# The last stores of a two-branch FNet and MLP layer: whole sets of four on one queue, the last chunk undivided, one sum moved behind a split

## The chip, the cores and the metric

The kernel runs on one core of one Trainium2 chip. The metric is the device time of one execution in microseconds (us); lower is better. The kernel before takes 862.84 us, the median of 3 runs (862.46 to 862.95).

## The reference: what is computed

For x of 2048 rows and 640 columns in float32, a layer norm feeds two branches, and all three terms are added:

```
xn = layernorm(x)
a, b = xn @ dft_hid_re.T, xn @ dft_hid_im.T
y = x + (dft_seq_re @ a - dft_seq_im @ b) + (gelu(xn @ w1 + b1) @ w2 + b2)
```

w1 is 640 by 1536, w2 is 1536 by 640, the sequence matrices are 2048 by 2048 and the hidden ones 640 by 640. All matrices are inputs, so the Fourier part is done with matmuls.

## The kernel before

**Numbers.** Every float32 operand is split into a high and a low part (`split`, lines 153 to 160): ScalarE copies the value into a rounded high part, VectorE subtracts that from the value to get the low part. A product is three matmuls (`product`, lines 268 to 273): high by high (line 271), high by low (line 272), low by high (line 273), accumulated in one PSUM bank. The weight operand is the stationary one, the split operand made by `form` (lines 490 to 504) the moving one, 512 columns wide.

**Stages.** First comes the MLP with the layer norm, over four blocks t of 512 rows. Its result plus x is kept in DRAM (`ys`). Then come the sequence stages, one for each of eight blocks (half h, rows t), and after every second block of the second half one hidden stage ("y") for a pair of row blocks `ta`, `tb`. Both kinds of stage form a product of 2 by 2 blocks with seven products (`NW = 7`) in place of eight. The last hidden stage is the end of the kernel; its pair is ta = 1, tb = 2.

**A hidden stage** has 21 entries n, seven products w by three units u. For each entry the main loop (lines 1229 to 1244) records the matmuls (`hidden_entry`, lines 1181 to 1223), then the functions in `pre`, then `form(n + 3)`, which splits the moving operand of the third entry from there, then the functions in `post`. Every engine runs its own instructions in that recorded order (`manual_schedule`). `hidden_beside` (lines 1053 to 1161) says what stands in `pre` and `post` of each entry.

In the last stage the last product (w = 6) is laid out differently (lines 1194 to 1204). Entry 18 holds 15 matmuls into bank VS (five positions of three) and then 15 into bank X; entry 19 holds 15 into bank X + 1; entry 20 holds none. Bank X already holds the sum after w = 5. That sum is read by VectorE at entry 17: `v1 += x_` (line 1123, recorded at line 407, 128x1024 over banks X and X + 1). The 15 matmuls into VS read the splits of entries 18, 19 and 20, two positions each of the first two and one of the third; the split for entry 20 is half as wide (128x512) and is the last form of the kernel.

**The results of the last stage** leave in this order. `out_b(0)` and `out_b(1)` (line 1115) store columns 0 to 63 and 64 to 127 of each quarter of block tb, from tiles `u`; `yb4` (line 1119) stores the odd 32 columns of tb from tile `y`; and after the main loop (lines 1252 to 1262) the third and fourth chunk of 32 columns of block ta leave tile `yo`. Each time VectorE turns a PSUM bank or a sum in 32 by 32 pieces (lines 842, 845, 1260) and adds the turned tile to what is in SBUF (line 407).

**A store** is `store` (lines 820 to 825): four DMAs, one for each quarter q of the partitions and of the columns. With `both` false all four are issued by SP (`nc.sync`), with `both` true the first two by SP and the last two by ACT (`nc.scalar`). Before the change `out_b(0)` goes to SP, all that follow use both. The last chunk is turned, added and stored in two halves of its row groups (`n0`, `n1`), each in four DMAs of 32 KB; the other stores of 32 columns are four of 64 KB, those of 64 columns four of 128 KB.

**Semaphores of DMAs.** Each DMA gets one of eight completion semaphores, here called 0 to 7. A DMA that gets one that was used before waits, in its queue, until the DMA that had it has landed; what is queued behind it on that engine waits as well. As the program is built, the last stores have these semaphores, in the order of each queue:

| store | SP before | ACT before | SP after | ACT after |
|---|---|---|---|---|
| `u`, columns 0 to 63 | 0, 1, 3, 5 | - | 0, 1, 3, 5 | - |
| `u`, columns 64 to 127 | 7, 2 | 2, 4 | - | 2, 4, 6, 1 |
| `y`, odd columns | 6, 1 | 6, 0 | 7, 0, 2, 3 | - |
| `yo`, third chunk | 2, 3 | 1, 3 | - | 4, 6, 0, 1 |
| `yo`, fourth chunk, first half | 4, 5 | 4, 5 | - | - |
| `yo`, fourth chunk, second half | 6, 7 | 7, 0 | - | - |
| `yo`, fourth chunk whole | - | - | 5, 7 | 2, 3 |

Where both queues of the kernel before have a semaphore in the same row (2, 6, 3, 4, 5, 7), the store on ACT has it first and that on SP waits for it; the SP store of `y` with semaphore 1 waits for the first `yo` store on ACT.

Of the kernel before, what the change touches and what calls it, by code (L numbers as in the profile page):

```python
# [16 lines left out]
Q = 4  # L17
B = 32
# [7 lines left out]
def kernel(  # L26
# [38 lines left out]
    nc = tc.nc  # L65
    x = x.flatten_outer_dims()
    out = out.flatten_outer_dims()
# [4 lines left out]
    NB = TB // B  # L72
# [4 lines left out]
    DQ = D // Q  # L77
# [27 lines left out]
    def bank(k):  # L105
        return banks[:, k]
# [35 lines left out]
    def place(tag, shape, dtype=F32R):  # L142

        return wpool.tile(list(shape), dtype, tag=tag, bufs=1, name=tag)
# [24 lines left out]
    def rows_of(ap, t):  # L169
        return ap[t * TB : (t + 1) * TB].rearrange("(n r) d -> r n d", r=B)  # L170
# [162 lines left out]
    A = {}  # L333
# [72 lines left out]
    def add(dst, a, b, op=ALU.add):  # L406
        nc.vector.tensor_tensor(dst, a, b, op=op)  # L407
# [23 lines left out]
    def load_a(g):  # L431

        for f in steps_of_load(g):
            f()
# [71 lines left out]
    def f5(u):  # L506
        add(held("ci1", u), held("ci1", u), held("ci2", u))

    def f6(u):
        add(held("cr1", u), held("cr1", u), held("ci1", u))  # L510
# [104 lines left out]
    for tag, size, keys in PLACES:  # L615
        t = place(tag, (P, size // 4))
# [13 lines left out]
    last = 1  # L630
# [99 lines left out]
    for g in range(NG):  # L730
        t, i = divmod(g, NF)
# [73 lines left out]
    def load_part(t, k):  # L805
        nc.sync.dma_start(new_sum(1, t, k), part_of(t, k))

    def gather(h, t, k, acc, first=False, op=ALU.add):

        if h == 0 and first:  # L810
            nc.scalar.activation(new_sum(h, t, k), acc, AF.Copy, scale=-1.0 if op == ALU.subtract else 1.0)
        else:
            add(sums[t, k], sums[t, k], acc, op)
# [3 lines left out]
            for k in names:  # L817
                nc.sync.dma_start(part_of(t, k), sums[t, k])

    def store(t, src, c0, c1, both=False, n0=0, n1=NB):  # L820

        for q in range(Q):
            (nc.scalar if both and q > 1 else nc.sync).dma_start(
                rows_of(out, t)[:, n0:n1, q * DQ + c0 : q * DQ + c1], src[q * B : (q + 1) * B, n0:n1]
            )

    def reload(lo, w, which="xab"):
# [10 lines left out]
    def turned(acc, name):  # L838

        if len(acc.shape) == 2:  # L840
            yt = A["yt"](name)[:, 0]
            nc.vector.transpose(yt, acc)
        else:
            yt = A["yt"](name)
            nc.vector.transpose(yt.rearrange("p e n -> p (e n)"), acc.rearrange("p e n -> p (e n)"))
        return yt

    def add_turned(dst, yt):
        if len(yt.shape) == 2:
            add(dst, dst, yt.rearrange("p (n i) -> p n i", i=B))  # L850
        else:
            d = dst.rearrange("p n (e i) -> p e n i", i=B)
            add(d, d, yt.rearrange("p e (n i) -> p e n i", i=B))
# [14 lines left out]
    X, Y, Z, US, VS = 0, 3, 5, 2, 7  # L868
    yo = {}
# [166 lines left out]
    def load_g(b, i):  # L1036
        if i >= NW * ND:
            return
        w, c = G[i]
        n = GWIDE[w] * P  # L1040
        places = A["g", b]
        k = i % len(places)
        if b < len(blocks) - 1 and w == NW - 1:

            k = (i - 2) % len(places)
            if c in CHUNKS[0]:
                k = CHUNKS[0].index(c)
                places = {k: fr_tile((P, 6 * P), f"u{2 - k}_{sets[blocks[b]]}", f"gr{k}_{b}", F32R)}
        g = places[k][:, : 2 * n].rearrange("p (a b) -> p a b", a=2)
        GT[b, i] = g  # L1050
        nc.sync.dma_start(g.bitcast(F32), wits[w][c])

    def hidden_beside(b, n):


        ta, tb = blocks[b - 1][1], blocks[b][1]
        last = b == len(blocks) - 1
        x_, y_, z_ = (banks[:, k : k + 2] for k in (X, Y, Z))
        us, vs = bank(US), bank(VS)
        ya = yo[ta]  # L1060

        def s(which, k):
            return sums[(ta, tb)[which], k]

        def t2(k):
            return lambda: add(s(1, KU[k]), s(1, KV[k]), s(1, KU[k]), ALU.subtract)

        def t3(k):
            return lambda: add(s(0, KU[k]), s(1, KU[k]), s(0, KU[k]), ALU.subtract)

        def t4(k):
            return lambda: add(s(0, KV[k]), s(0, KV[k]), s(1, KU[k]), ALU.subtract)

        def columns(k):

            return s(1 if last else 0, ("u1", "u2")[k]).rearrange("p a b -> p (a b)").rearrange("p (n e) -> p n e", n=NB)

        def load_yb(k):
            return lambda: nc.sync.dma_start(columns(k), ys[k][tb])

        def copy(dst, src):
            return lambda: nc.scalar.activation(dst, src, AF.Copy)

        def to(dst, acc, name, then=lambda: None):


            def f():
                add_turned(dst, turned(acc, name))
                then()

            return f

        def out_a(c0, c1):
            return lambda: store(ta, ya[:, :, c0:c1], c0, c1) if last else None

        def odd():
            yt = turned(us, f"yo_{tb}")
            add_turned(ya[:, :, 4 * B :], yt)
            add_turned(yo[tb, 4], yt)
            out_a(4 * B, DQ)()  # L1100

        def in_two(k):

            acc, name = s(1, ("v2", "v1")[k]), f"yb{k}_{tb}"

            def f():
                if name not in A:
                    A[name] = turned(acc, name)
                else:
                    add_turned(columns(k), A.pop(name))  # L1110
                    out_b(k)()

            return f

        def out_b(k):
            return lambda: store(tb, columns(k), 2 * k * B, 2 * (k + 1) * B, last and k == 1)

        yb1, yb2 = in_two(0), in_two(1)
        yb4 = to(yo[tb, 4], vs, f"yb4_{tb}", lambda: store(tb, yo[tb, 4], 4 * B, DQ, last))
        f5s = [lambda u=u: f5(u) for u in range(2)] if not last else [lambda: None] * 2  # L1120
        f6s = [lambda u=u: f6(u) for u in range(2)] if not last else [lambda: None] * 2
        pre = {
            17: [lambda: add(s(1, "v1"), s(1, "v1"), x_)],
        }.get(n, [])
        post = {

            0: [lambda: gather(1, tb, "v1", z_), lambda: gather(1, tb, "v", vs, op=ALU.subtract), f5s[0]],
            1: [f5s[1]],
            3: [to(ya[:, :, : 2 * B], x_, f"ya1_{ta}")],
            4: [t2(0)],  # L1130
            5: [t2(1)],
            6: [to(ya[:, :, : 2 * B], y_, f"ya2_{ta}", out_a(0, 2 * B)), t2(2)],
            7: [odd],
            8: [t3(0)],
            9: [copy(s(1, "v1"), z_), t3(1)],
            10: [t3(2)],
            11: [t4(0)],
            12: [copy(s(1, "v2"), x_), t4(1)],
            13: [load_yb(0), t4(2), load_yb(1)] if last else [t4(2)],
            14: [lambda: add(s(1, "v2"), s(1, "v2"), z_), yb1],  # L1140
            15: [yb1] if last else [load_yb(0)],
            16: [] if last else [load_yb(1)],
            17: [yb2, yb2] if last else [yb1, yb2],
            18: [yb4] if last else [yb2],
            19: [f6s[0]],
            20: [] if last else [f6s[1], yb4],
        }.get(n, [])
        if not last:
            if n in (12, 13):
                post.insert(0, lambda: load_g(b, (NW - 1) * ND + 13 - n))  # L1150
            if n == 18:
                post[:0] = [lambda k=k: load_part(blocks[b + 1][1], k) for k in ("u1", "u")]
            if n == 20:
                post.append(lambda: load_a(put_off[0]))

                def end():
                    to(ya[:, :, 2 * B : 4 * B], x_, f"ya3_{ta}")()
                    store(ta, ya, 0, DQ)

                later.append(end)  # L1160
        return pre, post
# [64 lines left out]
    for kind, what in stages:  # L1226
        b = blocks.index(what) if kind == "s" else b
        count = NW * (2 if kind == "s" else 3)
        for n in range(first, first + count):
            w, u = entries[n][2:]  # L1230
            if kind == "s":
                sequence_entry(n, what, w, u)
                pre, post = beside(*what, n - first)
            else:
                hidden_entry(n, b, w, u)
                pre, post = hidden_beside(b, n - first)
# [9 lines left out]
        if n + 1 < len(entries):  # L1246
            X, Y, Z = Y, Z, X
# [2 lines left out]


    t = blocks[-2][1]
    y = yo[t]
    add_turned(y[:, :, 2 * B : 3 * B], turned(bank(X), "yt_2"))
    store(t, y[:, :, 2 * B : 3 * B], 2 * B, 3 * B, True)
    yt = A["yt"]("yt_last")[:, 0].rearrange("p (n i) -> p n i", i=B)
    d, a = y[:, :, 3 * B : 4 * B], bank(X + 1).rearrange("p (n i) -> p n i", i=B)
    for n0 in (0, NB // 2):
        rows_ = slice(n0, n0 + NB // 2)
        nc.vector.transpose(yt[:, rows_], a[:, rows_])  # L1260
        add(d[:, rows_], d[:, rows_], yt[:, rows_])
        store(t, d, 3 * B, 4 * B, True, n0, n0 + NB // 2)


# [29 lines left out]
```

## Time and profile before

| what | value |
|---|---|
| median of 3 runs | 862.84 us |
| the profiled execution's own time | 862.57 us |
| its span, first to last instruction | 860.8 us |
| PE busy (TensorE matmul) | 851.1 us, 99% |
| DVE busy (VectorE) | 622.6 us, 72% |
| ACT busy (ScalarE) | 335.4 us, 39% |
| DMA queues q1 and q10, share of 16 engines | 62.1% and 4.3% |
| granted TensorE clock | 0.999 |

Times in the profile run from the start of the span. PE is the matmuls, PEld the weight loads in front of them, SPq and ACTq the DMA issues of SP and ACT. In the timeline a row has start, duration, engine, line, operation, what it writes and reads and how many it merges; in brackets stands the idle time before it and what ended it. In the list of DMA issues the last number is the median time from the issue to the landing.

### The profile page before, as it was taken

Reading aid. Unit: us, or ns where it says so; the run is one execution under the profiler, and the core shown is the slowest. Engines: PE = TensorE matmul, PEld = TensorE weight load, DVE = VectorE, ACT = ScalarE, POOL = GpSimd, SP = SyncE. Lnnn points to the kernel's source line nnn. Section 1 sums busy time; section 2 is a strip of 40 time slices with the busy share of each in tenths; the row PEclk is TensorE's granted clock in tenths of the full one; section 3 lists DMA queues with packets and bytes.
Section 4 is the critical chain, followed back from the end, with each engine's and each line's share of the span. In section 5 each row is a group of like instructions: output and inputs, shape, how many; then the busy total and the mean of one; then the engine's idle time right before and its main releaser. Section 6 shows DMA issues by size and latency. Waiting matters only on the chain.

```text
span 860.8 us, 10244 instructions
## 1 busy us (share of the span) xinstructions
PE 851.1 (99%) x3751; PEld 703.2 (82%) x3751; DVE 622.6 (72%) x788; ACT 335.4 (39%) x467; POOL 21.0 (2%) x22
## 2 busy tenths in 40 slices
PE   8999999999999999999999999999999999999996
PEld 6888888888888888888888888888888888888885
DVE  6554555366443678989989787998977998885596
ACT  6444434245333555443434344232322423222241
POOL 0000300030003000000000000000000000000000
PEclk9999999999999999999999999999999999999999
DMA  6747486876566984949753659954765879804464
GB/s 189 216 135 180 88 185 180 218 152 178 151 164 153 321 360 85 220 104 216 169 148 86 184 165 279 216 125 108 189 178 167 261 183 229 303 19 177 124 188 85
DMA packets 208689, 152.34 MB, mean 177 GB/s; under 512 B 82432, under 2 KB 183040, under 8 KB 208128
## 3 DMA queue, kind: packets, MB, share of 16 engines
q1 hardware_dynamic: 197136, 138.59, 62.1%
q10 hardware_dynamic: 11504, 13.11, 4.3%
q8 instruction: 29, 0.48, 0.2%
q14 instruction: 20, 0.16, 0.1%
HBM read 108.67 MB, written 42.99 MB: 176 GB/s over the span
## 4 chain that ended last, share of the span: by engine, by line
PE 98%; DVE 1%; DMA 1%; ACT 0%; issue 0%; SPq 0%; DVEq 0%; ACTq 0%
PE banks L272 26%; PE banks L273 26%; PE banks L271 26%; PE banks L289 19%; DMA x<-in_A_x_dram 1%; PE banks L627 0%; DVE st L184 0%; DVE yo L407 0%; DVE yt_last L1260 0%; DVE xp L207 0%; ACT xt L159 0%; DVE mv L185 0%; SPq L177 0%; ACT mv L191 0%; DVE mv L193 0%
## 5 line engine op out<-in xcount | busy, mean ns | idle before, releaser
L272 PE MATMUL banks<-as,xab 128*128 128x512 f32 x407 | 158.5, 389 | 0.0
L271 PE MATMUL banks<-as,xab 128*128 128x512 f32 x407 | 158.3, 389 | 0.0
L273 PE MATMUL banks<-as,xab 128*128 128x512 f32 x407 | 158.3, 389 | 0.0
L159 ACT ACTIVATE as<-r 128x1024 fp32r<-128x1024 f32 x80 | 85.0, 1062 | 173.5 <-PE banks L273 148.7
L160 DVE TENSOR_TENSOR as<-r,as 128x1024 fp32r<-128x1024 f32 x80 | 97.2, 1216 | 38.9 <-ACT as L159 38.9
L289 PE MATMUL banks<-xt,xab 128*128 128x512 f32 x420 | 99.2, 390 | 0.2 <-ACT xt L159 0.2
L304 DVE TENSOR_TENSOR hs<-ab,hs 128x512 fp32r<-128x512 f32 x48 | 36.5, 761 | 83.3 <-ACT hs L302 83.3
L289 PEld LDWEIGHTS banks<-xt,xab 128*128 128x128 f32 x420 | 78.4, 188 | 17.3 <-ACT xt L159 1.3
L272 PEld LDWEIGHTS banks<-as,xab 128*128 128x128 f32 x407 | 76.4, 188 | 16.3 <-DVE as L160 0.5
L271 PEld LDWEIGHTS banks<-as,xab 128*128 128x128 f32 x407 | 76.4, 188 | 15.9
L273 PEld LDWEIGHTS banks<-as,xab 128*128 128x128 f32 x407 | 76.4, 188 | 15.8
L271 PE MATMUL banks<-as,xc 128*128 128x512 f32 x224 | 87.1, 389 | 0.0
L272 PE MATMUL banks<-as,xc 128*128 128x512 f32 x224 | 87.1, 389 | 0.0
L273 PE MATMUL banks<-as,xc 128*128 128x512 f32 x224 | 87.1, 389 | 0.0
L298 ACT ACTIVATE ab<-banks,b1c 128x512 f32<-128x512 f32 x48 | 33.1, 689 | 99.7 <-PE banks L289 97.1
L159 ACT ACTIVATE as<-rt 128x1024 fp32r<-128x1024 f32 x32 | 34.0, 1063 | 70.1 <-PE banks L273 57.9
L289 PE MATMUL banks<-xt,as 128*128 128x512 f32 x240 | 57.0, 389 | 0.0
L289 PEld LDWEIGHTS banks<-xt,as 128*128 128x128 f32 x240 | 45.0, 188 | 9.4
L273 PEld LDWEIGHTS banks<-as,xc 128*128 128x128 f32 x224 | 42.0, 188 | 8.8
L271 PEld LDWEIGHTS banks<-as,xc 128*128 128x128 f32 x224 | 42.0, 188 | 8.7
L272 PEld LDWEIGHTS banks<-as,xc 128*128 128x128 f32 x224 | 42.0, 188 | 8.7
L271 PE MATMUL banks<-hs,xc 128*128 128x512 f32 x120 | 46.7, 389 | 0.0
(167 smaller groups left out, 1364.5 us busy)
## 6 DMA issues: line engine op xcount, KB each, us to landing
raw<-in_A_dft_seq_re_dram SPq DMA_DIRECT2D x64, 256.0 KB, 5.8
raw<-in_A_dft_seq_im_dram SPq DMA_DIRECT2D x64, 256.0 KB, 5.1
wit<-wst ACTq DMA_DIRECT2D x20, 384.0 KB, 3.2
ws<-wit SPq DMA_DIRECT2D x15, 384.0 KB, 5.1
xs<-x SPq DMA_DIRECT2D x64, 80.0 KB, 1.8
xo<-in_A_x_dram SPq DMA_DIRECT2D x16, 320.0 KB, 5.9
forms_ab<-xab SPq DMA_DIRECT2D x4, 1280.0 KB, 6.2
xab<-wit SPq DMA_DIRECT2D x13, 384.0 KB, 4.4
```

What stands on the lines that cost most here:

```text
L159: nc.scalar.activation(h, s, AF.Copy)
L160: nc.vector.tensor_tensor(l, s, h.bitcast(F32), op=ALU.subtract)
L271: nc.tensor.matmul(acc, wh, mh, start=first, stop=False, skip_group_check=goes_on)
L272: nc.tensor.matmul(acc, wh, ml, start=False, stop=False, skip_group_check=goes_on)
L273: nc.tensor.matmul(acc, wl, mh, start=False, stop=last, skip_group_check=goes_on)
L289: nc.tensor.matmul(acc, W1[i][:, a, j * P : (j + 1) * P], XT[j][:, b], start=n == 0, stop=n == len(steps) - 1)
L298: nc.scalar.activation(a, acc, AF.Gelu_apprx_tanh, bias=b1c[:, i : i + 1])
L304: nc.vector.tensor_tensor(hs[:, 1], a, hs[:, 0].bitcast(F32), op=ALU.subtract)
```

## The change

`store` takes the number of quarters that go to ACT instead of the switch `both`, and loses the row range. The second `u` store goes to ACT whole, `y` to SP whole, the third chunk to ACT whole. The fourth chunk is turned, added and stored once, two quarters on each queue. In the last hidden stage the sum `v1 += x_` of entry 17 goes from `pre`, ahead of `form(20)`, to `post`, behind it; in the earlier hidden stage it stays. On VectorE the low half of the last form so comes ahead of that sum and not behind it. All instructions ahead of these are the same in the same order.

```diff
-    def store(t, src, c0, c1, both=False, n0=0, n1=NB):
+    def store(t, src, c0, c1, on_act=0):
 
         for q in range(Q):
-            (nc.scalar if both and q > 1 else nc.sync).dma_start(
-                rows_of(out, t)[:, n0:n1, q * DQ + c0 : q * DQ + c1], src[q * B : (q + 1) * B, n0:n1]
+            (nc.scalar if q >= Q - on_act else nc.sync).dma_start(
+                rows_of(out, t)[:, :, q * DQ + c0 : q * DQ + c1], src[q * B : (q + 1) * B]
             )
...
-            return lambda: store(tb, columns(k), 2 * k * B, 2 * (k + 1) * B, last and k == 1)
+            return lambda: store(tb, columns(k), 2 * k * B, 2 * (k + 1) * B, Q if last and k == 1 else 0)
...
-        yb4 = to(yo[tb, 4], vs, f"yb4_{tb}", lambda: store(tb, yo[tb, 4], 4 * B, DQ, last))
+        yb4 = to(yo[tb, 4], vs, f"yb4_{tb}", lambda: store(tb, yo[tb, 4], 4 * B, DQ))
...
-        pre = {
-            17: [lambda: add(s(1, "v1"), s(1, "v1"), x_)],
-        }.get(n, [])
+        v1 = lambda: add(s(1, "v1"), s(1, "v1"), x_)
+        pre = [v1] if n == 17 and not last else []
...
-            17: [yb2, yb2] if last else [yb1, yb2],
+            17: [v1, yb2, yb2] if last else [yb1, yb2],
...
-    y = yo[t]
-    add_turned(y[:, :, 2 * B : 3 * B], turned(bank(X), "yt_2"))
-    store(t, y[:, :, 2 * B : 3 * B], 2 * B, 3 * B, True)
-    yt = A["yt"]("yt_last")[:, 0].rearrange("p (n i) -> p n i", i=B)
-    d, a = y[:, :, 3 * B : 4 * B], bank(X + 1).rearrange("p (n i) -> p n i", i=B)
-    for n0 in (0, NB // 2):
-        rows_ = slice(n0, n0 + NB // 2)
-        nc.vector.transpose(yt[:, rows_], a[:, rows_])
-        add(d[:, rows_], d[:, rows_], yt[:, rows_])
-        store(t, d, 3 * B, 4 * B, True, n0, n0 + NB // 2)
+    for k, on_act in ((2, Q), (3, Q // 2)):
+        d = yo[t][:, :, k * B : (k + 1) * B]
+        add_turned(d, turned(bank(X + k - 2), f"yt_{k}"))
+        store(t, d, k * B, (k + 1) * B, on_act)
```

## The prediction, made before the changed kernel ran

> **What bounds the kernel now.** I read the page first: busy shares, then the chain that ended last.
>
> ```profile
> span 860.8 us, 10244 instructions
> ...
> PE 851.1 (99%) x3751; PEld 703.2 (82%) x3751; DVE 622.6 (72%) x788; ACT 335.4 (39%) x467; POOL 21.0 (2%) x22
> ...
> PE 98%; DVE 1%; DMA 1%; ACT 0%; issue 0%; SPq 0%; DVEq 0%; ACTq 0%
> ...
> L272 PEld LDWEIGHTS banks<-as,xab 128*128 128x128 f32 x407 | 76.4, 188 | 16.3 <-DVE as L160 0.5
> ```
>
> TensorE carries the span: 98% of the chain. The chain ends with the last instruction of a compute engine, so the stores behind it are not in it. Two things can move: a stall of PE, and what follows PE's last matmul. The group of line 272 names one stall, 0.5 us on a low half from line 160. The timeline of the end shows where it is:
>
> ```profile
> 843.14 0.39 PE L272 MATMUL banks<-as,xab 128*128 128x512 f32 x1
> ...
> 843.73 1.22 DVE L160 TENSOR_TENSOR as<-v,as 128x1024 fp32r<-128x1024 f32 x1
> 843.80 0.63 ACT L159 ACTIVATE as<-v 128x512 fp32r<-128x512 f32 x1 [0.29 <-PE banks L273]
> ...
> 844.86 1.22 DVE L407 TENSOR_TENSOR v<-v,banks 128x1024 f32<-128x1024 f32 x1
> ...
> 846.00 0.69 DVE L160 TENSOR_TENSOR as<-v,as 128x512 fp32r<-128x512 f32 x1
> ...
> 846.32 0.39 PE L271 MATMUL banks<-as,xab 128*128 128x512 f32 x1
> 846.60 1.24 DVE L845 STREAM_TRANSPOSE yb<-v 128x1024 f32<-128x1024 f32 x1
> 846.73 0.19 PEld L272 LDWEIGHTS banks<-as,xab 128*128 128x128 f32 x1 [0.45 <-DVE as L160]
> ...
> 847.30 0.40 PE L271 MATMUL banks<-as,xab 128*128 128x512 f32 x1
> ...
> 850.94 0.72 DVE L842 STREAM_TRANSPOSE yt<-banks 128x512 f32<-128x512 f32 x1 [0.30 <-PE banks L273]
> ...
> 853.92 0.39 PE L273 MATMUL banks<-as,xab 128*128 128x512 f32 x1
> ...
> 854.34 0.45 DVE L1260 STREAM_TRANSPOSE yt_last<-banks 128x256 f32<-128x256 f32 x1 [1.96 <-PE banks L273]
> ```
>
> At 844.86 VectorE does the sum `v1 += x_` and only then, at 846.00, the low half of the last form, although ScalarE had its high half at 844.43. The fifth position of VS needs that low half, and PE waits. The other queues' rows tell of the second part: who issues the stores, and when. First SP, then ACT, then SP's waits.
>
> ```profile
> 843.84 2.04 SPq L823 DMA_DIRECT2D out_dram<-u  x4
> ...
> 849.12 2.71 SPq L823 DMA_DIRECT2D out_dram<-u  x2
> ...
> 852.59 2.02 SPq L823 DMA_DIRECT2D out_dram<-y  x2
> 854.71 0.99 SPq L823 DMA_DIRECT2D out_dram<-yo  x2
> ...
> 856.93 1.82 SPq L823 DMA_DIRECT2D out_dram<-yo  x4
> ```
>
> ```profile
> 849.13 0.93 ACTq L823 DMA_DIRECT2D out_dram<-u  x2
> 850.68 0.86 ACTq L823 DMA_DIRECT2D out_dram<-y  x2
> 852.42 0.86 ACTq L823 DMA_DIRECT2D out_dram<-yo  x2
> 855.28 1.87 ACTq L823 DMA_DIRECT2D out_dram<-yo  x4
> ```
>
> ```profile
> SPq L823 <- DMA out_dram<-yo: 2.7, 3, 1.4
> SPq L823 <- DMA out_dram<-u: 2.1, 1, 2.1
> ...
> SPq L823 <- DMA out_dram<-y: 0.7, 1, 0.7
> ```
>
> ACT issues each store about when its data is there. SP does not: it waits 2.1 + 2.7 + 0.7 = 5.5 us on earlier stores to land, because it shares their semaphores with ACT. Its two `yo` stores of the third chunk go out at 854.71, 2.3 us after ACT's at 852.42, and its four of the last chunk at 856.93, 1.7 us after ACT's first at 855.28 and 0.9 us after the last sum ended, which the next row gives as 856.07:
>
> ```profile
> 855.64 0.43 DVE L407 TENSOR_TENSOR yo<-yo,yt_last 128x256 f32<-128x256 f32 x1
> ```
>
> How long a store takes to land I asked for stretches that hold one store: its issue row, and below it its row in the list of DMA issues.
>
> ```profile
> 849.55 0.51 ACTq L823 DMA_DIRECT2D out_dram<-u  x1
> out_dram<-u ACTq DMA_DIRECT2D x1, 128.0 KB, 2.6
> ...
> 851.04 0.50 ACTq L823 DMA_DIRECT2D out_dram<-y  x1
> out_dram<-y ACTq DMA_DIRECT2D x1, 64.0 KB, 1.9
> ...
> 852.78 0.50 ACTq L823 DMA_DIRECT2D out_dram<-yo  x1
> out_dram<-yo ACTq DMA_DIRECT2D x1, 64.0 KB, 2.3
> ...
> 854.30 0.32 SPq L823 DMA_DIRECT2D out_dram<-y  x1
> out_dram<-y SPq DMA_DIRECT2D x1, 64.0 KB, 1.7
> ...
> 858.30 0.45 SPq L823 DMA_DIRECT2D out_dram<-yo  x1
> out_dram<-yo SPq DMA_DIRECT2D x1, 32.0 KB, 1.6
> ```
>
> So the last store lands at 858.30 + 1.6 = 859.9, and 0.9 us of final waits and barriers follow to 860.8.
>
> **Part 1, the sum behind the last form.** From 843.14 to 846.32 PE makes 14 matmuls in 3.18 us, 0.227 each. From 846.32 to 853.92 there are 32 more, which would take 7.26 us at that pace and take 7.60. The stall costs 0.34 us to the end of PE's work (0.30 in the three steps from 846.32 to 847.30, the rest in slightly slower ones after them). After the change the low half starts at 844.86 and, at 0.60 to the next start, the sum at 845.46 and ends near 846.68; the turn at 846.60 starts as before, since the two operations only change places. The low half is needed at 846.32 and there by 845.55: the stall goes. What is late next is the sum itself, since the first matmul into bank X must not write before the sum has read it. That matmul stands at 847.30 now and 0.30 earlier without the stall, at 847.00, its weight load near 846.77. PE was released 0.04 after the low half's end (846.69 to 846.73), so the sum releases near 846.72: 0.05 us in hand. Behind it wait the 30 matmuls that end the kernel, so each lateness is paid in full. Gain between 0 and 0.34, and no loss, since VectorE has the same work done by 846.60 in either order; I take 0.34, as no row puts the release later than the load's turn.
>
> **Part 2, the last sums.** PE's last bank is then ready at 854.34 - 0.34 = 854.00. The whole chunk is turned and summed like the third, from start to first issue 852.42 - 850.94 = 1.48 us: the last stores go out at 855.48. Before, the first half's went out at 855.28 and the second half's data was there at 856.07. Undividing costs 0.2 on the first half and gains 0.6 on the second, 0.34 of each being PE's.
>
> **Part 3, the queues.** Are both free at 855.48? SP: four `u` stores as before, then `y` at 850.68 in four, by the row of 843.84 in 2.04 us, to 852.7; its third waits for ACT's first `u` store, issued at 849.13 and landed by 851.8 even at 2.6. SP is free 2.8 us early. ACT: four `u` stores from 849.13 to 851.2, then the third chunk, ready 0.27 earlier than 852.42 (VectorE's 0.30 of waiting at 850.94 goes, as PE is 0.34 earlier), in four from 852.15. Its third waits for SP's second `y`, issued near 851.04 and landed by 853.4 at 2.3; behind it wait the fourth and ACT's last pair. It is done near 854.4, 1.1 us ahead. The last pair on ACT waits for SP's third and fourth `y`, issued by 852.2 and landed by 854.8 at 2.6. So nothing holds the last four stores, and moving whole sets costs nothing: 1.1 us of slack on ACT covers it, and beyond that each us late is a us of the end.
>
> The second store of each queue follows the first by 852.78 - 852.42 = 0.36 us: 855.84. The time to land is what the trace doesn't have for four stores of 64 KB at once. It lies between 1.7, a store alone, and 2.6, one of twice the size beside two others; the nearest is 2.3, one of 64 KB with another queue's beside it, of which 1.9 to 2.3 is the spread. I take 2.2: landed at 858.04, bounds 857.54 and 858.44.
>
> The Trainium skill (DMA: Bandwidth & Descriptors, Issuing engines are not separate DMA queues) says that DMAs of both queues run on the same 16 engines, so that issuing from two saves only issue time. By it, whole sets on one queue lose nothing but the issue time, which the slack above covers; the 2.04 us for four stores on SP agrees with that price.
>
> **The sum.** End = 858.04 + 0.9 = 858.9, against 860.8: 1.9 us less, of which 0.34 is PE's and some 1.6 the stores'. The bounds of the landing give 2.4 and 1.5 (a store of 64 KB at 1.7 lands 0.5 earlier, one at 2.6 lands 0.4 later). The profiled execution took 862.57 us, 0.27 below the median of 862.84. From the median: 862.84 - 1.9 = 860.9 us; bounds 860.4 and 861.3.
>
> **The rivals.**
>
> 1. *PE's wait takes another place.* The sum's release at 846.72 has 0.05 us in hand. If the first matmul into bank X waits as long as the old one did, or the old wait had another cause, 0.34 is lost: 861.3. For it: the thin margin. Against: the weight load of 846.73 follows the low half's end at once, and the stall cost PE less than its 0.45 of idle load, so a small lateness is absorbed.
>
> 2. *The four last stores run one behind another.* If descriptors for SP and ACT are made in turn, the fourth store starts not 0.36 but three issue steps after the first, 3 x 0.5 (2.04 / 4) = 1.5: the last landing is 1.1 later, the gain 0.8, the time 862.0. For it: `u` on ACT at 849.55, beside SP's, took 2.6 to land and the alone one at 854.30 1.7. Against: SP's issue at 849.12 and ACT's at 849.13 ran side by side, neither held up. The Trainium skill (Perfetto Trace Analysis, DMA Instruction — HWDGE) says that the block which makes the descriptors is shared by the two issuing sequencers and locked by one of them while it generates; by that rule this rival would hold, and the two issues side by side speak against its full price.
>
> 3. *ACT's queue falls behind (slower).* ACT now moves 4 x 128 + 6 x 64 = 896 KB in ten stores where it moved 640. Place: the eight stores ahead of its last pair. If each blocked its queue, the last pair would go out late. The end is 1.73 us (0.2%) later than now when the pair starts at 862.5 - 0.9 - 2.2 - 0.36 = 859.0, that is, eight stores in 9.9 us from 849.13, 1.24 each. The row of 843.84 has 0.51 each. At 1.3 the time would be 865.0.
>
> 4. *The change doesn't do what it says:* SP's waits stay because new pairs of semaphores tie the queues. As built, the only ties left are those three named in part 3, each met early. If one came at 856.9 as now, the gain would be PE's 0.34 and a little: 862.4. This is part of rival 2's chance.
>
> **How the numbers follow.** 0.2%, 1.73 us, is about what a measurement of this kernel can tell from no change. Forecast 76% (860.4 to 861.3, centre 860.9), of which a little under three quarters lies under 861.11; rival 1 10%; rivals 2 and 4 11%; rival 3 3%. Faster by over 0.2%: 0.76 x 0.74 = 0.56; slower 0.03; the rest, 0.41, within. The range reaches from the forecast's lower bound over rival 1 most of the way to rival 2: 860.4 to 861.8.
>
> **What would show it.** In the timeline after: no idle time on a weight load near 846.5, PE's last matmul at about 853.6, line 160 ahead of line 407 there. In SP's waits: nothing of the 5.5 us on stores. Four stores of 64 KB between 855.4 and 856.0, landed by 858.1 to 858.4, span near 858.9. Wrong would be: idle time before line 271 near 846.8 with line 407 named (rival 1); landings over 2.6 us or issues over 0.5 for the last four (rival 2); ACT issuing the last pair after 856 (rivals 3 and 4).

## The result, and the profile after

The changed kernel takes 861.35 us (median of 20 runs, 861.13 to 861.94), the one before 862.64 (20 runs, 862.40 to 863.54): 1.29 us or 0.15% less by the medians, ratio 0.9986 with a 95% interval of 0.9979 to 0.9992. The sign and the range (860.4 to 861.8) of the prediction held. The forecast gain was 1.9 us, the measured one 1.3, which falls on the other side of the 0.2% line (1.73 us).

The profiled execution after took 861.94 us with a span of 860.1, 0.6 above its median. Its chain of work still ends in PE:

```profile
span 860.1 us, 10233 instructions
...
PE 98%; DMA 1%; DVE 1%; ACT 0%; issue 0%; SPq 0%; DVEq 0%; ACTq 0%
```

The 0.6 does not come from the end. In the timeline of weight loads two have waited, at an earlier hidden stage, for nothing that the profile shows; the kernel before has none there in its profile:

```profile
680.50 0.19 PEld L271 LDWEIGHTS banks<-as,ws 128*128 128x128 f32 x1 [0.28 <-issue]
...
683.60 0.19 PEld L271 LDWEIGHTS banks<-as,gr_b 128*128 128x128 f32 x1 [0.51 <-issue]
```

Waits of 0.2 to 0.8 us in all stand near 170, 350 or 680 us in some profiles of these kernels and not in others; those near 170 and 350 have VectorE named as what ended them, those near 680 nothing. So absolute times of two profiles are not subtracted here. What can be compared is the **tail**: from VectorE's first turn of the last bank, which starts as PE's last matmul ends, to the end of the span. Before it is 860.78 - 854.34 = 6.4 us. After, the timeline has the two last sums, and the queues of SP and ACT:

```profile
844.35 1.82 DVE L160 TENSOR_TENSOR as<-v,as 128x1024 fp32r<-128x1024 f32 x2
846.09 1.22 DVE L407 TENSOR_TENSOR v<-v,banks 128x1024 f32<-128x1024 f32 x1
...
854.61 0.72 DVE L842 STREAM_TRANSPOSE yt<-banks 128x512 f32<-128x512 f32 x1 [1.68 <-PE banks L273]
855.36 0.69 DVE L407 TENSOR_TENSOR yo<-yo,yt 128x512 f32<-128x512 f32 x1
```

```profile
851.41 2.06 SPq L823 DMA_DIRECT2D out_dram<-y  x4
856.08 0.85 SPq L823 DMA_DIRECT2D out_dram<-yo  x2
```

```profile
849.87 2.08 ACTq L823 DMA_DIRECT2D out_dram<-u  x4
852.97 4.05 ACTq L823 DMA_DIRECT2D out_dram<-yo  x6
```

The two low halves now run in one piece at 844.35 and the sum follows at 846.09. No weight load waits there: around the place of the old stall, behind 846.93, the matmuls keep their step of 0.23, down to PE's last one.

```profile
846.71 0.39 PE L273 MATMUL banks<-as,xab 128*128 128x512 f32 x1
846.93 0.39 PE L271 MATMUL banks<-as,xab 128*128 128x512 f32 x1
847.16 0.39 PE L272 MATMUL banks<-as,xab 128*128 128x512 f32 x1
...
854.19 0.39 PE L273 MATMUL banks<-as,xab 128*128 128x512 f32 x1
```

From 846.93 to 854.19 the last 32 steps of PE take 7.26 us, where they took 7.60 before (846.32 to 853.92): the 0.34 of the stall is gone.

SP's last two stores go out at 856.08, 1.47 after the first turn, and none of its stores waits for another any more; among its waits only VectorE stands ahead of line 823, and the last two rows are the end of the program:

```profile
SPq L823 <- DVE u L407: 6.4, 1, 6.4
SPq L823 <- DVE y L407: 4.8, 1, 4.8
SPq L823 <- DVE yo L407: 2.5, 1, 2.5
SPq L1282 <- DMA out_dram<-yo: 2.1, 2, 1.4
SPq L1282 <- PEq L1282: 0.6, 2, 0.4
```

The tail is 860.15 - 854.61 = 5.5 us, 0.9 less than before. With PE's 0.34 that makes some 1.24, and the medians say 1.29. So the question left by the prediction is where 0.6 us went: it had 858.9 - 854.00 = 4.9 us for the tail.

### The profile page after: what moved, and what is told of

It is laid out like the page before. It is cut to its first block, busy times and chain, and to the rows that moved or that the text cites. A ratio compares the mean times of both kernels' runs of the same rounds, so it can differ in the third digit from the quotient of the medians.

```text
span 860.1 us, 10233 instructions
## 1 busy us (share of the span) xinstructions
PE 851.5 (99%) x3751; PEld 703.5 (82%) x3751; DVE 622.5 (72%) x786; ACT 335.9 (39%) x467; POOL 21.0 (2%) x22
## 4 chain that ended last, share of the span: by engine, by line
PE 98%; DMA 1%; DVE 1%; ACT 0%; issue 0%; SPq 0%; DVEq 0%; ACTq 0%
PE banks L271 26%; PE banks L273 26%; PE banks L272 26%; PE banks L289 19%; DMA x<-in_A_x_dram 1%; PE banks L627 0%; DVE st L184 0%; DVE yt L842 0%; DVE yo L407 0%; DVE xp L207 0%; ACT xt L159 0%; DVE mv L185 0%; SPq L177 0%; ACT mv L191 0%; DVE mv L193 0%
```

## The experiments

The theory (A) after the result: the stores gain because the last chunk's stores no longer wait on semaphores, and it is dividing that chunk that made them wait; the gain falls short because four stores at once land later than one alone, and because of what follows the landing. Rivals: the whole sets untied the queues (B); PE's part and the stores' part do not add; the third chunk's stores hold the last ones; descriptors are made in turn for both queues.

### Each part alone

**The sum alone.** The kernel before with

```diff
-        pre = {
-            17: [lambda: add(s(1, "v1"), s(1, "v1"), x_)],
-        }.get(n, [])
+        v1 = lambda: add(s(1, "v1"), s(1, "v1"), x_)
+        pre = [v1] if n == 17 and not last else []
...
-            17: [yb2, yb2] if last else [yb1, yb2],
+            17: [v1, yb2, yb2] if last else [yb1, yb2],
```

> The kernel before with only the sum moved behind the last form. The tail is the time from VectorE's first turn of the last bank to the end of the span; it is 6.4 us before (854.34 to 860.8) and 5.5 after (854.61 to 860.15). Theory (the two parts are independent; PE's stall is worth 0.34): no idle weight load near 846.5, tail still 6.4, SP still waits some 5.5 us on stores, time 862.3, 0.3 less than before. Rival (a stall removed is filled by slack in the stores, because SP is held by landings and not by PE): stall gone, tail 6.7, time unchanged at 862.6.

862.79 us, ratio 1.0004 (0.9995 to 1.0014): no gain. The stall is gone, and the first turn starts at 853.89 in place of 854.34. But the span is the same and the tail has grown to 6.9. The rival was right, and by more than it said. The timeline from the first turn on, VectorE's row first, then SP's and ACT's (the four of the last row are the last four of the six in SP's first), and then ACT's first half-store with SP's two neighbours in the list of DMA issues:

```profile
853.89 0.45 DVE L1259 STREAM_TRANSPOSE yt_last<-banks 128x256 f32<-128x256 f32 x1 [1.68 <-PE banks L273]
...
854.60 4.20 SPq L823 DMA_DIRECT2D out_dram<-yo  x6
...
854.83 0.32 ACTq L823 DMA_DIRECT2D out_dram<-yo  x1
...
857.00 1.80 SPq L823 DMA_DIRECT2D out_dram<-yo  x4
```

```profile
out_dram<-yo SPq DMA_DIRECT2D x2, 64.0 KB, 2.1
out_dram<-yo ACTq DMA_DIRECT2D x1, 32.0 KB, 2.1
```

ACT's first half-store goes out 0.45 earlier than before (854.83, was 855.28; PE has no wait at an earlier stage in either profile, and 0.34 of it is the stall), but takes 2.1 to land where it took 1.6, beside SP's two 64 KB stores that are still late from the third chunk. SP issues six stores from 854.60: two late ones, then the last four, which wait for ACT's landing and start at 857.00, when they started at 856.93 before. A faster PE only ran into SP's queue.

**The stores alone.** The changed kernel with

```diff
-        pre = [v1] if n == 17 and not last else []
+        pre = [v1] if n == 17 else []
...
-            17: [v1, yb2, yb2] if last else [yb1, yb2],
+            17: [yb2, yb2] if last else [yb1, yb2],
```

> The changed kernel with the sum back ahead of the last form: only the stores are changed. Theory: PE's stall is there again (0.45 idle on a weight load of line 272), tail 5.5, time 861.7, 0.9 less than before. Rival (the stores gain only together with the earlier end of PE): tail 5.9 or more, time over 862.0.

861.63 us, 1.0 less by the medians than before beside it on the same chip (862.61). The ratio, 0.9992 (0.9983 to 1.0001), says 0.7 and does not by itself exclude that nothing changed; what shows the gain is the tail. The old stall is there again, and the tail is 861.04 - 855.50 = 5.5, as in the changed kernel:

```profile
847.89 0.19 PEld L272 LDWEIGHTS banks<-as,xab 128*128 128x128 f32 x1 [0.45 <-DVE as L160]
```

So the stores are worth 0.9 by themselves by the tail, and the sum nothing by itself. On top of the stores the sum is worth 0.3 by the gains of 1.3 and 1.0, as the 0.34 of PE's end would have it; the two gains are of different chips, and their intervals do not part.

### Undivided chunk or whole sets

**Only the last chunk whole.** The kernel before with

```diff
-    for n0 in (0, NB // 2):
-        rows_ = slice(n0, n0 + NB // 2)
-        nc.vector.transpose(yt[:, rows_], a[:, rows_])
-        add(d[:, rows_], d[:, rows_], yt[:, rows_])
-        store(t, d, 3 * B, 4 * B, True, n0, n0 + NB // 2)
+    add_turned(y[:, :, 3 * B : 4 * B], turned(bank(X + 1), "yt_3"))
+    store(t, y[:, :, 3 * B : 4 * B], 3 * B, 4 * B, True)
```

> The kernel before with one edit: the last chunk is turned, added and stored whole, two quarters on each queue; all sets stay split over both queues and the sum stays ahead of the form. Theory A (undividing does it: with the third chunk's four and eight half stores there are twelve stores for eight semaphores, so some must wait for landings, and with four whole ones the waits fall on stores that landed long before): SP still waits on stores before the last chunk, some 4 us, but its two last stores go out within 0.1 of ACT's, tail 5.3 to 5.5, time 861.6. Rival B (whole sets on one queue are what unties the queues): SP's last two go out 0.7 or more behind ACT's, tail 6.2 to 6.4, time 862.4 to 862.6.

861.52 us, 1.1 less than before (0.9989, 0.9981 to 0.9998): the whole gain of the stores from this edit. SP still waits for landings, but what it waits for is over when the last sum ends. First SP's waits, then the timeline of the last chunk:

```profile
SPq L823 <- DMA out_dram<-u: 2.0, 1, 2.0
SPq L1284 <- DMA out_dram<-yo: 1.8, 2, 1.2
SPq L823 <- DMA out_dram<-yo: 1.1, 1, 1.1
```

```profile
854.36 0.72 DVE L842 STREAM_TRANSPOSE yt<-banks 128x512 f32<-128x512 f32 x1 [1.95 <-PE banks L273]
...
855.83 0.85 SPq L823 DMA_DIRECT2D out_dram<-yo  x2
...
855.84 0.93 ACTq L823 DMA_DIRECT2D out_dram<-yo  x2
```

Both queues issue 1.47 after the first turn, as in the changed kernel. With the chunk undivided, B has nothing left to explain: the whole sets add nothing here. What they do for a divided chunk is the next run's question.

**Whole sets, divided chunk.** The changed kernel, `store` with the row range again, and for the last chunk

```diff
-        add_turned(d, turned(bank(X + k - 2), f"yt_{k}"))
-        store(t, d, k * B, (k + 1) * B, on_act)
+    for n0 in (0, NB // 2):
+        rows_ = slice(n0, n0 + NB // 2)
+        nc.vector.transpose(yt[:, rows_], a[:, rows_])
+        add(d[:, rows_], d[:, rows_], yt[:, rows_])
+        store(t, d, 3 * B, 4 * B, Q // 2, n0, n0 + NB // 2)
```

> The changed kernel with the last chunk in two halves again, each two and two on the queues; sets whole on one queue and sum moved as in the changed kernel. As built, ACT's second half-store has the semaphore of SP's first one. Theory A: ACT's second store of the last chunk waits for SP's first to land, its last goes out 3.4 us after VectorE's first turn and lands 1.7 later, tail 5.9 to 6.1, time 861.9. Rival B: the queues are untied by the sets, the last half-store goes out 2.3 after the first turn and lands by 4.0, tail 4.9 to 5.1, time 860.9, faster than the changed kernel.

861.63 us, 1.0 less than before (862.61; 0.9989, 0.9980 to 0.9998), and a tail of 860.09 - 854.25 = 5.8, a little under what A said, and far from B's 4.9 to 5.1. ACT's third-chunk and half-stores in the timeline, one after another:

```profile
855.39 0.89 ACTq L823 DMA_DIRECT2D out_dram<-yo  x2
...
856.73 1.33 ACTq L823 DMA_DIRECT2D out_dram<-yo  x3
```

The first row is the third chunk's last store, held for a landing until 855.39, and the first half-store behind it, 0.6 after SP's, which went out at 855.19. The second half-store has the semaphore of SP's first, which landed 1.5 after its issue, at 856.7; it starts at 856.73. With sets whole and the sum moved, twelve stores on eight semaphores still tie the queues.

B is not wrong altogether, though. The right neighbour of this run is the sum alone, which differs from it only in the sets: there the tail is 6.9 and the time 862.79 on the same chip, here 5.8 and 861.63. There SP's last four stores begin 857.00 - 853.89 = 3.1 us after the first turn, here 855.19 - 854.25 = 0.9 (the row below), since SP no longer waits for ACT's landings. So with a divided chunk the whole sets take 1.1 us off the tail. Undividing alone takes off 1.6 (the tail is 5.35 in the best version below), and once that is done the whole sets take nothing further.

```profile
855.19 1.82 SPq L823 DMA_DIRECT2D out_dram<-yo  x4
```

### What is in the landing

**Two of the last four stores left out.** The changed kernel with

```diff
-        for q in range(Q):
+        for q in range(0, Q, step):
```

and a step of 2 for the last chunk, 1 for all other sets.

> The changed kernel without the second and the fourth quarter's store of the last chunk: these two are left out, so one store of 64 KB goes out on each queue. Theory (the four stores share the DMA engines: 2048 pieces of 128 bytes, which in the changed kernel land 2.0 to 2.6 after issue): both land 1.9 to 2.1 after issue, last landing 0.9 earlier against the first turn than in the changed kernel, tail 4.5 to 4.7. Rival (the third chunk's stores, landed only at 856.91, hold the last ones): landing stays at 2.2 or more, tail 4.9 to 5.2.

The first turn is at 854.77 and the span 859.5: a tail of 4.7. The two stores go out at 856.24. Their rows in the list of DMA issues:

```profile
out_dram<-yo SPq DMA_DIRECT2D x1, 64.0 KB, 2.0
out_dram<-yo ACTq DMA_DIRECT2D x1, 64.0 KB, 2.2
```

They land at 2.0 and 2.2. The 2.2 is still the rival's figure; the tail of 4.7 is the theory's, and the next run parts the two. In the changed kernel the second pair goes out 0.36 and 0.42 after the first store, as the timeline of SP and of ACT has it, and lands at 2.4 and 2.6 in the list of DMA issues:

```profile
856.44 0.49 SPq L823 DMA_DIRECT2D out_dram<-yo  x1
...
856.50 0.51 ACTq L823 DMA_DIRECT2D out_dram<-yo  x1
```

```profile
out_dram<-yo SPq DMA_DIRECT2D x1, 64.0 KB, 2.4
out_dram<-yo ACTq DMA_DIRECT2D x1, 64.0 KB, 2.6
```

**The third chunk's stores left out.** The changed kernel with

```diff
-        store(t, d, k * B, (k + 1) * B, on_act)
+        if k == 3:
+            store(t, d, k * B, (k + 1) * B, on_act)
```

> The changed kernel without the stores of the third chunk, which are left out. Theory (sharing among the four last stores): the last of them still lands 2.4 to 2.6 after its issue and 2.9 after the first's, tail 5.2 to 5.5 (ACT's last has semaphore 6, one of the last that SP reads, which saves up to 0.2). Rival (the third chunk's stores hold them): the last lands 2.0 to 2.2 after issue, tail 4.9 or less.

The second pair lands 2.4 and 2.6 after its issue, as with the third chunk's stores there, and the tail is 859.2 - 853.82 = 5.4. The rival that these stores hold the last ones falls.

```profile
853.82 0.72 DVE L842 STREAM_TRANSPOSE yt<-banks 128x512 f32<-128x512 f32 x1 [1.71 <-PE banks L273]
```

**All four on SP.** The changed kernel with

```diff
-    for k, on_act in ((2, Q), (3, Q // 2)):
+    for k, on_act in ((2, Q), (3, 0)):
```

> The changed kernel with all four stores of the last chunk on SP. Theory (issue steps of 0.4 to 0.55 on one queue count, both queues generate side by side): the fourth goes out 1.5 after the first and lands 2.0 to 2.2 later, 3.6 after the first issue against 2.99, tail 6.1. Rival 2 of the prediction (descriptors are made in turn for both queues anyway, or the 16 engines alone set the end): last landing 2.9 to 3.1 after the first issue, tail 5.5.

The result lies between the two: the tail is 860.1 - 854.18 = 5.9. SP's four issues and the last of them alone in the timeline, and the first and the last in the list of DMA issues:

```profile
855.65 1.95 SPq L823 DMA_DIRECT2D out_dram<-yo  x4
...
857.10 0.51 SPq L823 DMA_DIRECT2D out_dram<-yo  x1
```

```profile
out_dram<-yo SPq DMA_DIRECT2D x1, 64.0 KB, 1.7
...
out_dram<-yo SPq DMA_DIRECT2D x1, 64.0 KB, 1.9
```

The last goes out at 857.10 and lands at 859.0, 3.4 after the first issue against 3.0 (859.1 - 856.08) in the changed kernel. One queue issues its last 1.0 us later than two queues do, and loses only 0.4 of it, because each store then lands in 1.7 to 1.9. The windows show the difference: first the stretch in which the changed kernel moves this data, then that of this run. The columns are the stretch, its length, the busy engines, the granted clock, the share of the 16 DMA engines and GB/s:

```profile
856.92:858.49 1.57, 0.00 (x0) 0.00 (x0) 0.00 (x0) 0.00 (x0) 0.00 (x0) 0.50 1.04 167
```

```profile
856.49:858.62 2.13, 0.00 (x0) 0.00 (x0) 0.00 (x0) 0.00 (x0) 0.00 (x0) 1.00 0.72 123
```

With two queues the DMA engines are busy all through, at a share of 1.04 (packets overlap, so a share can pass 1), and move 256 KB in pieces of 128 bytes in 1.57 us; with one their share is 0.72. Whether the engines or the memory behind them set that pace is not shown.

**Three on SP and one on ACT**, on the kernel of the next experiment:

```diff
-    for k, on_act in ((2, Q), (3, Q // 2)):
+    for k, on_act in ((2, Q), (3, 1)):
```

> The kernel with the semaphores moved on by four (of the changed kernel's sets), and of the last chunk's stores three on SP and one on ACT. Theory (the 16 engines are the limit: 2048 pieces of 128 bytes took 1.57 us in the changed kernel however the queues share them): last landing 4.4 to 4.6 after the first turn, tail 5.25 to 5.4, time 861.1 to 861.2. Rival (stores of two queues slow each other and one queue alone lands each in 1.7 to 1.9): SP's third goes out 2.36 after the first turn and lands 1.95 later, 4.3, tail 5.1, time 860.9.

861.25 us, tail 859.33 - 853.91 = 5.4. SP's third store is the last to land:

```profile
856.27 0.51 SPq L823 DMA_DIRECT2D out_dram<-yo  x1
```

```profile
out_dram<-yo SPq DMA_DIRECT2D x1, 64.0 KB, 2.1
```

It lands at 858.4, 4.5 after the first turn, as in the changed kernel; the rival had 4.3. So the last landing does not move when the stores are dealt out three and one.

### What follows the landing

**Semaphores moved on by four.** The changed kernel with the load `yo[t, 4]` of the last sequence stage in five DMAs:

```diff
-                    nc.sync.dma_start(yo[t, 4], ys[2][t])
+                    cuts = [0, 3, 6, 10, 13, 16] if p == 3 else [0, NB]
+                    for lo, hi in zip(cuts, cuts[1:]):
+                        nc.sync.dma_start(yo[t, 4][:, lo:hi], ys[2][t][:, lo:hi])
```

> The changed kernel with one earlier load, that of the odd columns of block tb in the last sequence stage, cut into five DMAs, so that all later semaphores move on by four: ACT's last two stores have 6 and 7 in place of 2 and 3. SP reads the final semaphores in a fixed order that ends with 7. Theory (the store that lands last is read second in the changed kernel and four reads of 0.06 follow): from the last landing to the end 0.83 in place of 1.08, tail 5.25, time 861.1, 0.25 less than the changed kernel. Rival (the reads are hidden behind barriers of other engines): 1.08 stays, time 861.35.

861.13 us (862.82 before; 0.9979, 0.9970 to 0.9988). The first turn starts at 854.41 and the span is 859.7, a tail of 5.3. ACT's last pair in the timeline:

```profile
855.88 0.93 ACTq L823 DMA_DIRECT2D out_dram<-yo  x2
```

The second goes out at 855.88 + 0.93 - 0.51 = 856.30 and lands 2.6 later by the list of DMA issues, at 858.9, as far behind the first turn as in the changed kernel (4.5). From there to the end it is 0.8, where the changed kernel has 860.15 - 859.1 = 1.0 to 1.1; the rival, which kept that, falls. The changed kernel's five reads behind its last landing stand in the view of the program's last line:

```profile
L1282 SPq EVENT_SEMAPHORE  x5: 28/28/28, 859.1 to 859.3; - x5
```

They begin with the semaphore that lands last and start within 0.25 us (859.09 to 859.34); moved on by four, that semaphore is the last of them. On one chip with the changed kernel:

> The changed kernel itself, on the chip of the two others. Both theories: 1.3 us less than the kernel before, 861.35, no stall near 846.5, tail 5.5, of which 1.08 follows the last landing.

> The kernel with the semaphores moved on by four, beside the changed kernel on one chip. Theory (order of the final reads): 0.25 less than the changed kernel, 861.1, tail 5.29. Rival (the 0.22 seen before was the other chip): the same time as the changed kernel within 0.1.

861.57 us for the changed kernel (862.72 before; 0.9985, 0.9976 to 0.9994) and 861.33 for the other (0.9983, 0.9975 to 0.9992), tails 5.54 and 5.29 again, within 0.01 of those on the other chips. The sign is the same on both occasions and the tails say 0.25; the intervals of the two kernels' times do not part by themselves.

### The best version

**The last chunk whole and the sum moved**, nothing else: the diffs of "The sum alone" and of "Only the last chunk whole" together, on the kernel before.

> The kernel before with two edits: the last chunk whole, and the sum behind the last form; every set but the first stays split over both queues. Theory A (with the last chunk whole nothing ahead of it holds the queues, so an earlier end of PE reaches the end; whole sets on one queue add nothing): no stall near 846.5, tail 5.3 to 5.4, as fast as the changed kernel or up to 0.2 faster, 861.2. Rival (the split sets hold SP by landings as in the kernel with the sum alone): tail 5.7, time 861.5, as with the whole chunk alone.

861.05 us (0.9982, 0.9973 to 0.9991), 1.7 less than before and 0.5 less than the changed kernel beside it on the same chip. The tail is 5.35: VectorE's first turn at 854.12, both queues' issues at 855.59, a span of 859.5.

```profile
854.12 0.72 DVE L842 STREAM_TRANSPOSE yt<-banks 128x512 f32<-128x512 f32 x1 [1.71 <-PE banks L273]
...
855.59 0.93 ACTq L823 DMA_DIRECT2D out_dram<-yo  x2
```

As built, ACT's last store has semaphore 6 here, read next to last, and 0.9 us follow its landing. That is 0.2 of the 0.5; the rest is about the size of the waits at 350 and 680 us that come and go between executions, but that it is these is not shown, and the intervals of the two runs overlap.

## Why the prediction was right or wrong, point by point

- **Part 1, the sum behind the last form: right as a mechanism, wrong as a term that can be added.** The stall went, no wait took its place at bank X (rival 1 fell), and PE's end came earlier by the 0.34 (7.26 us in place of 7.60). The sum alone gave nothing, though, since SP's landings and not PE set the end before. On top of the freed stores it is worth some 0.3, which the times do not show clear of noise; PE's rows do. The step that added it held only because the stores were freed in the same change.
- **Part 2, the last sums: right.** 1.48 us from the first turn to the first store were forecast, 1.47 measured.
- **Part 3, the queues: right in its times, not in its reason.** Both queues were free when the last sum ended, as said. ACT's margin was smaller: its third store of the third chunk waited until 854.62, as SP's second `y`, issued at 851.77, took 2.8 to land where I had 2.3, and the fourth was issued by 854.62 + 0.86 = 855.5, 0.6 us ahead and not 1.1:

```profile
854.62 0.86 ACTq L823 DMA_DIRECT2D out_dram<-yo  x2
```

Undividing the last chunk was enough to free its stores; the whole sets, to which I gave the same gain, do most of it as well when the chunk stays divided, and nothing more when it does not. I read SP's 5.5 us of waits as one loss; the run with only the chunk whole keeps 3.1 of them and loses nothing by it.
- **Part 3, the landing: the mis-sized term.** "I take 2.2" measured 2.6, at the upper bound. The rows that I weighed were of stores that overlapped in part; the four overlap wholly and keep the DMA engines busy all through (1.04). The step from first to second store was 0.42 on ACT in place of 0.36. Together this is some 0.4 of the missing 0.6.
- **The end: mis-sized.** I carried 0.9 us over from the kernel before. There the last landing has semaphore 7, read last; after the change it has 3, read second. That is the other 0.2. The order of the reads stands in the built program and could have been read there.
- **Rival 2** (the last stores one behind another) was right in part: what they share is the 16 DMA engines, and it cost some 0.4, not 1.1. The Trainium skill (DMA: Bandwidth & Descriptors, Issuing engines are not separate DMA queues) has that rule, that a second queue saves only issue time; the run on SP alone agrees, with 0.4 us of a 1.0 us issue saving left at the end. The rows that I held for this rival, 2.6 against 1.7, were of a store of 128 KB and one of 64 KB, so size was mixed in. The Trainium skill's rule of a locked descriptor block (Perfetto Trace Analysis, DMA Instruction — HWDGE) shows here, if at all, as 0.06 us: ACT's first issue of the last pair started beside SP's at 856.08 and took 0.38, one with none of SP's beside it 0.32.

```profile
854.62 0.32 ACTq L823 DMA_DIRECT2D out_dram<-yo  x1
...
856.09 0.38 ACTq L823 DMA_DIRECT2D out_dram<-yo  x1
```

- **Rivals 3 and 4** did not come about. The gain of 1.3 lies between the forecast's lower bound of 1.5 and rival 2's 0.8, inside the range, but the chance of 0.56 for more than 0.2% rested on the landing.
- **The range held with some luck.** The time of 861.35 lies just past the forecast's own upper bound of 861.3; it is inside only because the range was stretched towards rival 2. And the kernel before came out 0.2 lower in 20 runs (862.64) than in the 3 that the forecast started from (862.84), so the time is off by 0.45 where the gain is off by 0.6.

## What to carry to other kernels

Count the transfers in flight at the end against the semaphores that they share: when there are more, cutting a store in two to start it earlier can make one queue wait for the other, and a faster engine ahead of it gains nothing until that is gone. Leaving the store whole or giving whole sets to one queue each removed most of that here, and the two do not add. A store's time to land is to be read from a stretch where as many bytes of that piece size are in flight as will be; the four stores of 128-byte pieces ended at the same time dealt out two and two or three and one, and 0.4 us later all on one queue. And the transfer that lands last should have the semaphore that the end of the program reads last, here worth 0.25 us of the tail.

## What the runs showed of the hardware that was not expected

Two stores of 64 KB issued together on SP and ACT land in 2.0 and 2.2 us where one alone takes 1.7 (at 854.30 before, and the first of the run on SP alone), so already two slow each other. The reads of landed semaphores at the end start 0.06 us apart (0.25 for four), one after another. And in some executions of one and the same kernel PE idles 0.2 to 0.8 us in all at earlier stages, those near 680 us put down to nothing by the profile; their cause stays open.
